# A first mixture with its elementwise steps laid out one by one, its differences on VectorE, and x loaded a second time, moved by a token

## The chip, the cores and the metric

The kernel runs on one core of one Trainium2 chip. The metric is device time in microseconds (us) of one launch. Engines: TensorE (PE; PEld is its weight load), VectorE (DVE), ScalarE (ACT), GpSimd (POOL), and SyncE (SP), whose queue issues most transfers.

## The reference, cut to what matters

```
attn  = relu(z zT / S)**2 @ v;  x = u * attn          # 4 x 3072 tokens, 256 wide
x_prev = x moved by one token, zero at the start of each sequence
xk = mu_k * x + (1 - mu_k) * x_prev
xr = mu_r * x + (1 - mu_r) * x_prev
k  = relu(xk @ w_k);  y = sigmoid(xr @ w_r) * (k * k @ w_v)   # the first mixture, 1024 wide inside
out = ((y @ w_a) * (y @ w_b)) @ w_out                  # the second mixture, 1536 wide inside
```

Everything is fp32 in and out. Weights arrive as 64-bit floats and are decoded in the kernel.

## The kernel before

Three stages follow each other: the attention, the first mixture, the second mixture. TensorE multiplies in fp32r, and each fp32 factor is split into a rounded part (hi) and a rest (lo), so that one product is three matmuls (hi hi, hi lo, lo hi: `mm3`, and the loop in `product`). A split is a copy to fp32r (`hi`, ScalarE) and a difference (`lo`, VectorE).

Tokens are taken in blocks of QB = 512 (24 of them; `i`), and the first mixture in pairs of blocks (NP = 12; `j`). The product with w_k of a pair is done by seven products in place of eight (`PRODUCTS`): the four blocks of xk (b11, b21 of the first token block, b12, b22 of the second) and four differences t1 to t4 (`value` in `operands`, tile `tv`) are split into seven `k_t` operands. A pair has UN = 4 units (`unit(u)`), each with 128 x 2 of the 1024 inner columns. A unit has seven products on PSUM banks `px`, `pw`, `py` (21 matmuls), the sums of banks that give `c1` and `c2`, relu and square, their splits (`kh`, `kl`), one gate (`gate`, bank `pg`, 6 matmuls, then a sigmoid), and, one unit later, four `net` calls (24 matmuls) that multiply k*k by w_v into four accumulators `vacc`. `result` multiplies them by the gate and stores y. A full unit thus has 51 matmuls; the first has no nets of a unit before it.

`net` 0 and 1 need the halves of `c1`, `net` 2 and 3 those of `c2`.

All of it is issued in an order written by hand (`tc.manual_schedule`): each engine and each DMA queue runs its instructions in the order of the program, and waits by semaphores for tiles. The elementwise work that prepares pair j + 1 is hung into the units of pair j: `side[(u, t)]` holds functions that `tick(t)` calls at eight places of unit u. Before, `steps` puts whole lists there, one entry per tick: `key_values` (xk: ScalarE forms (1 - mu) * x_prev by a copy with a scale, lines L523 and L525 for the column from the block before, VectorE adds mu * x, L530), `operands`, and `gate_values` (the same for xr, then the split `mix`). GpSimd (`SIDE`) computes the differences `tv` (L746) and the `lo` of `mix` (L569). For pair 0 the same work is hung into the end of the attention (`at(base - 22 + n, ...)`; the index counts half-units, and `base` is where the mixture begins).

Storage: `gp` (`g_tile`) has 25 buffers of 4 KB per partition for weights, operands of pair 0, x, the gates and half of the `mix` tiles, and for the attention's tiles ahead of that; `late` (`late_tile`) 18; `wp` (`w_tile`) 6, for `c1`, `c2`, `kh`, `kl`; `cp` (`c_tile`) 5 of 2 KB; `stp` 3; PSUM 4 banks `ps` and 4 accumulators. A tile takes a buffer when one is free, and its first writer waits for the last reader of the tile that had it.

The second mixture has 144 units of 33 matmuls, and prepares each next pair of blocks by the same `operands`, one list of steps per unit from its sixth unit on.

Of the kernel before, what the change touches and what calls it, by code (L numbers as in the profile page):

```python
# [16 lines left out]
P = 128  # L17
# [8 lines left out]
TICKS = 8  # L26
# [3 lines left out]
def tile_kernel(  # L30
# [60 lines left out]
    om = const.tile([P, 2, ND], F32, name="om")  # L91
# [19 lines left out]
    SIDE = nc.gpsimd  # L111
# [389 lines left out]
    mix_t, xk_t, k_t, sig_t = {}, {}, {}, {}  # L501
# [9 lines left out]
    def x_load(i):  # L511
        b, s = divmod(i, NQB)
        x_t[i] = g_tile([P, ND, QB], F32, "xs")
        nc.sync.dma_start(x_t[i], x_kept[b][:, :, s * QB : (s + 1) * QB])

    def mixed(i, c, d, dst):

        st = {}

        def before():  # L520
            x = x_t[i]
            st["t"] = t = c_tile(F32, "mt")
            nc.scalar.activation(t[:, 1:], x[:, d, : QB - 1], AF.Copy, scale=om[:, c, d : d + 1])  # L523
            if i % NQB:
                nc.scalar.activation(t[:, 0:1], x_t[i - 1][:, d, QB - 1 :], AF.Copy, scale=om[:, c, d : d + 1])  # L525
            else:
                nc.vector.memset(t[:, 0:1], 0.0)

        def both():
            nc.vector.scalar_tensor_tensor(  # L530
                dst(), x_t[i][:, d, :], mu[:, c, d : d + 1], st["t"], op0=ALU.mult, op1=ALU.add
            )

        return before, both

    def key_values(i):


        def dst(d):
            def fn():  # L540
                if d == 0:
                    xk_t[i] = stp.tile([P, ND, QB], F32, tag="st", name="xk")
                return xk_t[i][:, d, :]

            return fn

        (b0, m0), (b1, m1) = (mixed(i, 0, d, dst(d)) for d in range(ND))
        return [[b0], [m0, b1], [m1]]

    def gate_values(i):  # L550

        make = late_tile if i % 2 else g_tile
        st = {}

        def dst(d):
            def fn():
                if d == 0:
                    st["m"] = stp.tile([P, ND, QB], F32, tag="st", name="xr")
                return st["m"][:, d, :]

            return fn

        def high():
            mix_t[i] = [make([P, ND, QB], F32R, f"mix{h}") for h in range(2)]
            nc.scalar.activation(mix_t[i][0], st["m"], AF.Copy)

        def low():
            hi, lo = mix_t[i]
            SIDE.tensor_tensor(lo, st["m"], hi.bitcast(F32), op=ALU.subtract)  # L569

        (b0, m0), (b1, m1) = (mixed(i, 1, d, dst(d)) for d in range(ND))
        return [[b0], [m0, b1], [m1], [high], [low]]

    def mixture1():
        side = {}
        back = {}

        def steps(u, first, todo):
            for n, fns in enumerate(todo):
                v, t = divmod(first + n, TICKS)  # L580
                side.setdefault((u + v, t), []).extend(fns)

        def gate(u):

            j, f = divmod(u, UN)
            i, g = 2 * j + f // ND, f % ND
# [4 lines left out]
            pg = ps_tile("pg")  # L591
# [3 lines left out]
            nc.scalar.activation(sig_t[i][:, g, :], pg, AF.Sigmoid)  # L595

        def net(u, k):
# [6 lines left out]
            for d in range(ND):  # L604
# [469 lines left out]
```

## Time and profile before

| what | value |
|---|---|
| median of 3 runs | 2637.17 us (2634.65 to 2638.5) |
| the profiled execution | 2636.18 us, its span 2634.3 us |
| mean granted clock of TensorE | 0.998 |
| busy: PE, DVE, ACT, POOL | 99%, 74%, 63%, 11% |
| attention, first mixture, second mixture | 0 to 963, 963 to 1532, 1532 to 2634 us of the span |

A busy PE is not one at its peak, since matmuls overlap; the distance from one instruction's start to that of the next is the better measure. Idle time of another engine matters only where TensorE waits for it.

### The profile page before, as it was taken

What the parts mean: (1) busy time and instruction counts of PE and PEld (TensorE: products, weight loads), DVE (VectorE), ACT (ScalarE), POOL (GpSimd) and SP (SyncE); (2) the same over time, 40 slices, a digit from 0 to 9 for tenths busy, and PEclk for the clock granted to TensorE, in tenths of its full rate; (3) what the DMA queues carried; (4) which work ended last, traced back from release to release, by engine and by line L of the source; (5) the groups of instructions that cost most, each with busy time, mean ns of one, the idle gap of its engine ahead of it and who ended that gap; (6) DMA issues with size and microseconds to landing.
All of it is one profiled execution on the core that took longest, in us unless ns stands there. A gap on an engine that the chain in (4) does not pass through costs nothing.

```text
span 2634.3 us, 31196 instructions
## 1 busy us (share of the span) xinstructions
PE 2599.1 (99%) x11424; PEld 2132.1 (81%) x11424; DVE 1958.0 (74%) x2723; ACT 1665.3 (63%) x2380; POOL 281.8 (11%) x249
## 2 busy tenths in 40 slices
PE   8999999999999999999999999999999999999998
PEld 6888888888888877778878788888888888888887
DVE  7887877778778778788787767766676767677665
ACT  7867876787687667777777644444544444444443
POOL 0000100001001022222222200000000000000000
PEclk9999999999999999999999999999999999999999
DMA  7787779768968860110101340011011101110100
GB/s 208 210 231 187 222 222 235 209 188 251 214 182 240 222 178 33 49 48 33 64 32 36 137 172 25 9 33 33 1 33 32 33 1 32 33 25 9 32 17 17
DMA packets 254681, 274.14 MB, mean 104 GB/s; under 512 B 173632, under 2 KB 185920, under 8 KB 246848
## 3 DMA queue, kind: packets, MB, share of 16 engines
q1 hardware_dynamic: 234704, 175.68, 27.5%
q0 software_dynamic: 17712, 95.95, 9.5%
q8 instruction: 89, 1.46, 0.2%
q10 hardware_dynamic: 2112, 0.52, 0.1%
q14 instruction: 64, 0.52, 0.1%
HBM read 151.00 MB, written 121.11 MB: 103 GB/s over the span
## 4 chain that ended last, share of the span: by engine, by line
PE 88%; DVE 5%; ACT 2%; issue 2%; DMA 1%; SPq 0%; DVEq 0%; ACTq 0%
PE px L864 14%; PE acc L103 9%; PE acc L104 9%; PE acc L105 9%; PE py L864 7%; PE oacc L104 5%; PE oacc L105 5%; PE oacc L103 5%; PE pw L864 3%; PE px L631 3%; PE sc L357 3%; PE sc L358 3%; PE vacc L104 2%; PE vacc L105 2%; PE vacc L103 2%; PE py L631 2%
## 5 line engine op out<-in xcount | busy, mean ns | idle before, releaser
L104 PE MATMUL acc<-lo,vhi 128*128 128x512 f32 x1152 | 449.2, 390 | 1.6 <-DVE lo L419 1.6
L103 PE MATMUL acc<-hi,vhi 128*128 128x512 f32 x1152 | 450.0, 391 | 0.0
L105 PE MATMUL acc<-hi,vlo 128*128 128x512 f32 x1152 | 449.1, 390 | 0.0
L864 PE MATMUL px<-t,w 128*128 128x512 f32 x1296 | 364.2, 389 | 0.1
L848 ACT ACTIVATE abh<-cc 128x512 fp32r<-128x512 f32 x288 | 182.5, 634 | 282.8 <-DVE cc L930 254.1
L864 PEld LDWEIGHTS px<-t,w 128*128 128x128 f32 x1296 | 243.1, 188 | 51.4 <-ACT c L906 0.5
L924 DVE TENSOR_TENSOR c<-py,c 128x512 f32<-128x512 f32 x144 | 99.5, 691 | 235.9 <-ACT c L906 235.9
L104 PEld LDWEIGHTS acc<-lo,vhi 128*128 128x128 f32 x1152 | 216.7, 188 | 47.6 <-DVE lo L419 2.3
L105 PEld LDWEIGHTS acc<-hi,vlo 128*128 128x128 f32 x1152 | 216.6, 188 | 45.2
L103 PEld LDWEIGHTS acc<-hi,vhi 128*128 128x128 f32 x1152 | 216.7, 188 | 44.9
L370 ACT ACTIVATE p<-sc 128x1024 f32<-128x1024 f32 x167 | 171.1, 1024 | 117.2 <-PE sc L358 115.4
L377 DVE STREAM_TRANSPOSE pt<-p 128x512 f32<-128x512 f32 x240 | 156.4, 690 | 106.6 <-ACT p L371 102.1
L104 PE MATMUL oacc<-abl,w 128*128 128x512 f32 x572 | 223.7, 391 | 5.7 <-DVE abl L849 5.7
L105 PE MATMUL oacc<-abh,w 128*128 128x512 f32 x572 | 222.7, 389 | 0.0
L103 PE MATMUL oacc<-abh,w 128*128 128x512 f32 x572 | 222.6, 389 | 0.0
L906 ACT ACTIVATE c<-px 128x512 f32<-128x512 f32 x144 | 86.0, 597 | 214.7 <-PE px L864 214.7
L849 DVE TENSOR_TENSOR abl<-cc,abh 128x512 fp32r<-128x512 f32 x288 | 211.8, 736 | 0.1
L419 DVE TENSOR_TENSOR lo<-p,hi 128x1024 fp32r<-128x1024 f32 x167 | 199.6, 1195 | 5.1 <-PE pz L265 0.5
L371 ACT ACTIVATE p<-p 128x1024 f32<-128x1024 f32 x167 | 177.1, 1061 | 5.3
L419 DVE TENSOR_TENSOR lo<-pm,hi 128x1024 fp32r<-128x1024 f32 x120 | 147.1, 1227 | 33.1 <-ACT hi L416 32.7
L930 DVE SCALAR_TENSOR_TENSOR cc<-px,cc 128x512 f32<-128x512 f32 x144 | 99.5, 691 | 93.9 <-PE px L864 93.9
L104 PE MATMUL vacc<-kl,w 128*128 128x512 f32 x384 | 151.0, 393 | 0.5 <-DVE kl L641 0.5
(131 smaller groups left out, 5289.1 us busy)
## 6 DMA issues: line engine op xcount, KB each, us to landing
pkept<-pt POOLq DMA_DIRECT2D x60, 1024.0 KB, 5.9
pm<-pkept SPq DMA_DIRECT2D x240, 256.0 KB, 6.1
kept<-w POOLq DMA_DIRECT2D x39, 512.0 KB, 5.5
w<-kept SPq DMA_DIRECT2D x39, 512.0 KB, 8.6
vst<-in_v SPq DMA_DIRECT2D x24, 512.0 KB, 7.3
ust<-in_u SPq DMA_DIRECT2D x192, 64.0 KB, 4.4
xkept<-x POOLq DMA_DIRECT2D x24, 512.0 KB, 5.3
xs<-xkept SPq DMA_DIRECT2D x24, 512.0 KB, 5.6
```

Of the source, the lines that this page charges most:

```text
L103: nc.tensor.matmul(ps, wh, ah, start=first, stop=False)
L104: nc.tensor.matmul(ps, wh, al, start=False, stop=False)
L105: nc.tensor.matmul(ps, wl, ah, start=False, stop=last)
L370: nc.scalar.activation(p, sc, AF.Relu, scale=1.0 / S)
L371: nc.scalar.activation(p, p, AF.Square)
L377: nc.vector.transpose(pt[:, :, 2 * pr + t, :], p[:, t, :].rearrange("p (c i) -> p c i", i=SQ))
L419: nc.vector.tensor_tensor(l, p, h.bitcast(F32), op=ALU.subtract)
L631: nc.tensor.matmul(bank, w[x][:, c], t[:, y, :], start=first and m == 0, stop=end and m == 2, skip_group_check=True)
L848: return (lambda: nc.scalar.activation(h, p, AF.Copy)), (lambda: nc.vector.tensor_tensor(l, p, h.bitcast(F32), op=ALU.subtract))
L849: lambda: nc.vector.tensor_tensor(l, p, h.bitcast(F32), op=ALU.subtract)
L864: nc.tensor.matmul(bank, w[x][:, c], t[:, y, :], start=first and m == 0, stop=end and m == 2, skip_group_check=True)
L924: nc.vector.tensor_tensor(c22, y, c22, op=ALU.add)
```

## The change

In the first mixture:
- x of a block is loaded twice, as it is (`xs`) and moved by one token (`xp`; zero in the first column of a sequence). `change` takes xp from xs in place, and `mixed` forms xp + mu * (x - xp) in one VectorE instruction for each half. The copies with a scale (L523, L525) and the tile `om` go.
- `prepare(j)` lists every step with the unit and the tick at which it is issued. For pair 0 the 32 steps follow each other, one per half-unit, from `base - 33`.
- The differences `tv` and the `lo` of `mix` move from GpSimd to VectorE. `operands`, shared with the second mixture, changes in the same way there.
- In a unit, the order of work between the products changes (gate first, then nets by three, three and two). `c12` and `c22` are tiles of `cp`; bank y is copied by ScalarE after product 5, and x7 is added to it in one VectorE instruction. Relu, square and split of `c2` are issued in the next unit (`late`). The casts `kh` move from VectorE to ScalarE.
- The banks are asked for in an order that turns with the unit (`BANKS`).
- The gates of pair 0 all stand in unit 0, three of them on accumulators; sigmoids are issued some steps after their gate.

```diff
...
-    om = const.tile([P, 2, ND], F32, name="om")
...
-    SIDE = nc.gpsimd
...
+    mix_t, xk_t, xr_t, k_t, sig_t, p_t = {}, {}, {}, {}, {}, {}
...
     def x_load(i):
...
+        x_t[i], p_t[i] = (g_tile([P, ND, QB], F32, n) for n in ("xs", "xp"))
...
+        if s:
+            nc.sync.dma_start(p_t[i], x_kept[b][:, :, s * QB - 1 : (s + 1) * QB - 1])
+        else:
+            nc.vector.memset(p_t[i][:, :, 0:1], 0.0)
+            nc.sync.dma_start(p_t[i][:, :, 1:], x_kept[b][:, :, : QB - 1])
+    def change(i):
+        nc.vector.tensor_tensor(x_t[i], x_t[i], p_t[i], op=ALU.subtract)
+    def mixed(i, c, d):
+        t = (xk_t, xr_t)[c]
+        if d == 0:
+            t[i] = stp.tile([P, ND, QB], F32, tag="st", name=("xk", "xr")[c])
+        nc.vector.scalar_tensor_tensor(
+            t[i][:, d, :], x_t[i][:, d, :], mu[:, c, d : d + 1], p_t[i][:, d, :], op0=ALU.mult, op1=ALU.add
+        )
+    def gate_high(i, make):
+        mix_t[i] = [make([P, ND, QB], F32R, f"mix{h}") for h in range(2)]
+        nc.scalar.activation(mix_t[i][0], xr_t[i], AF.Copy)
+    def gate_low(i):
+        hi, lo = mix_t[i]
+        nc.vector.tensor_tensor(lo, xr_t[i], hi.bitcast(F32), op=ALU.subtract)
...
     def mixture1():
...
+        sigmoid = []
+        BANKS = (("px", "pw", "py", "pg"), ("pg", "px", "py", "pw"), ("pw", "pg", "py", "px"))
+        def gate(u, f, bank):
+            i, g = 2 * (u // UN) + f // ND, f % ND
...
+            pg = bank or accp.tile([P, QB], F32, tag="acc", name="vacc")
...
+            sigmoid.append(lambda: nc.scalar.activation(sig_t[i][:, g, :], pg, AF.Sigmoid))
+        def net(u, k, d):
...
+            first, last = f == 0 and k < 2, f == UN - 1 and k > 1
+            if first:
+                acc[n, d] = accp.tile([P, QB], F32, tag="acc", name="vacc")
+            c = slice(f * D + d * P, f * D + (d + 1) * P)
+            mm3(acc[n, d], wh[:, c], wl[:, c], hi, lo, first, last)
+            if last and d == ND - 1:
...
+            if prev < 0:
+                between = [[lambda g=g: gate(u, g, None if g else pg)] for g in range(UN)]
+            else:
+                nets = [lambda k=k, d=d: net(prev, k, d) for k in range(4) for d in range(ND)]
+                if j:
+                    between = [[lambda: gate(u, f, pg)], nets[:3], nets[3:6], nets[6:]]
+                else:
+                    between = [nets[:2], nets[2:4], nets[4:6], nets[6:]]
+            def gap(n):
+                for fn in between[n]:
+                    fn()
...
+            banks = {n: ps_tile(n) for n in BANKS[u % len(BANKS)]}
+            x, w, y, pg = (banks[n] for n in ("px", "pw", "py", "pg"))
+            relu, square, high, low = back[prev]["late"] if prev >= 0 else [lambda: None] * 4
             product(x, 1, True, False)
             product(w, 2, True, True)
...
             product(y, 5, True, False)
...
+            relu()
+            c1 = w_tile(F32, "c1")
+            c12, c22 = c_tile(F32, "c12"), c_tile(F32, "c22")
             nc.scalar.activation(c1[:, 0, :], x, AF.Copy)
             nc.vector.tensor_tensor(c1[:, 0, :], w, c1[:, 0, :], op=ALU.add)
+            square()
+            nc.scalar.activation(c22, y, AF.Copy)
             tick(0)
...
+            gap(0)
+            high()
             tick(1)
             product(x, 6, False, False)
-            nc.scalar.activation(c2[:, 0, :], x, AF.Copy)
+            nc.scalar.activation(c12, x, AF.Copy)
+            low()
+            if sigmoid:
+                sigmoid.pop(0)()
             tick(2)
...
+            gap(1)
+            while sigmoid:
+                sigmoid.pop(0)()
             tick(3)
             product(x, 7, False, False)
-            nc.scalar.activation(c1[:, 1, :], x, AF.Copy)
-            nc.vector.tensor_tensor(c1[:, 1, :], y, c1[:, 1, :], op=ALU.add)
+            nc.vector.tensor_tensor(c1[:, 1, :], x, c22, op=ALU.add)
             tick(4)
...
+            nc.scalar.activation(c1, c1, AF.Relu)
+            nc.scalar.activation(c1, c1, AF.Square)
+            gap(2)
+            while sigmoid:
+                sigmoid.pop(0)()
             tick(5)
             product(x, 4, False, True)
             product(y, 3, False, True)
...
+            c2 = w_tile(F32, "c2")
             nc.scalar.activation(c2[:, 1, :], x, AF.Relu)
...
+            h1 = w_tile(F32R, "kh")
+            nc.scalar.activation(h1, c1, AF.Copy)
+            nc.vector.tensor_tensor(c2[:, 0, :], y, c12, op=ALU.add)
             tick(6)
...
-            nc.vector.tensor_copy(h1, c1)
...
+            l1 = w_tile(F32R, "kl")
+            nc.vector.tensor_tensor(l1, c1, h1.bitcast(F32), op=ALU.subtract)
+            gap(3)
+            while sigmoid:
+                sigmoid.pop(0)()
             tick(7)
...
-            nc.vector.tensor_copy(h2, c2)
...
+            def relu():
+                nc.scalar.activation(c2[:, 0, :], c2[:, 0, :], AF.Relu)
+            def square():
+                nc.scalar.activation(c2, c2, AF.Square)
+            def high():
+                h = back[u]["h2"] = w_tile(F32R, "kh")
+                nc.scalar.activation(h, c2, AF.Copy)
+            def low():
+                h, l = back[u]["h2"], w_tile(F32R, "kl")
+                nc.vector.tensor_tensor(l, c2, h.bitcast(F32), op=ALU.subtract)
+                hl[0, 1], hl[1, 0] = (h[:, 0, :], l[:, 0, :]), (h[:, 1, :], l[:, 1, :])
...
+            back[u]["late"] = relu, square, high, low
...
+                for fn in back[u]["late"]:
+                    fn()
+                for k in range(4):
+                    flush.append(lambda k=k: [net(u, k, d) for d in range(ND)])
+        def prepare(j):
+            i0, i1 = 2 * j, 2 * j + 1
+            value, hi, lo = operands(k_t, j, lambda n: xk_t[2 * j + n], late_tile if j else g_tile)
+            odd = late_tile if j else g_tile
+            return [
+                (0, 0, lambda: change(i0)),
+                (0, 1, lambda: mixed(i0, 0, 0)),
+                (0, 3, lambda: mixed(i0, 0, 1)),
+                (1, 1, lambda: change(i1)),
+                (1, 1, hi["b11"]),
+                (1, 2, lambda: mixed(i1, 0, 0)),
+                (1, 3, lambda: mixed(i1, 0, 1)),
+                (1, 3, hi["b21"]),
+                (1, 4, value["t1"]),
+                (1, 5, lo["b11"]),
+                (1, 5, hi["t1"]),
+                (1, 6, value["t2"]),
+                (1, 7, lo["t1"]),
+                (2, 0, value["t4"]),
+                (2, 0, hi["t2"]),
+                (2, 1, lo["b21"]),
+                (2, 1, hi["t4"]),
+                (2, 2, value["t3"]),
+                (2, 2, hi["b22"]),
+                (2, 3, lo["t2"]),
+                (2, 3, hi["t3"]),
+                (2, 4, lo["t4"]),
+                (2, 5, lo["b22"]),
+                (2, 6, lo["t3"]),
+                (3, 0, lambda: mixed(i0, 1, 0)),
+                (3, 1, lambda: mixed(i0, 1, 1)),
+                (3, 2, lambda: mixed(i1, 1, 0)),
+                (3, 2, lambda: gate_high(i0, g_tile)),
+                (3, 3, lambda: mixed(i1, 1, 1)),
+                (3, 4, lambda: gate_high(i1, odd)),
+                (3, 5, lambda: gate_low(i0)),
+                (3, 6, lambda: gate_low(i1)),
+            ]
...
+        at(base - 40, lambda: x_load(0))
+        at(base - 39, lambda: x_load(1))
+        for n, (_, _, fn) in enumerate(prepare(0)):
+            at(base - 33 + n, fn)
+        at(base - 3, lambda: x_load(2))
+        for j in range(1, NP):
...
+            if j > 1:
+                side.setdefault((u - 1, 4), []).append(lambda j=j: x_load(2 * j))
+            side.setdefault((u, 4), []).append(lambda j=j: x_load(2 * j + 1))
+            for v, t, fn in prepare(j):
+                side.setdefault((u + v, t), []).append(fn)
+        u = (NP - 1) * UN
+        side.setdefault((u, 4), []).append(lambda: y_load(0))
+        value, hi, lo = operands(t_t, 0, lambda n: y_t[0][n], lambda *a: (g_tile if a[2] == "b22" else late_tile)(*a))
+        for v, t, fn in (
...
+        ):
+            side.setdefault((u + v, t), []).append(fn)
...
     def operands(t_t, j, source, make):
...
-                SIDE.tensor_tensor(val[name], a(), b(), op=ALU.subtract)
+                nc.vector.tensor_tensor(val[name], a(), b(), op=ALU.subtract)
...
+        return {"t1": t1, "t2": t2, "t3": t3, "t4": t4}, hi, lo
...
+                value, hi, lo = operands(
...
+                steps = [
+                    [value["t1"], hi["b11"], hi["t1"]],
+                    [lo["b11"], lo["t1"], hi["b21"]],
+                    [value["t2"], lo["b21"], hi["t2"]],
+                    [lo["t2"], value["t4"], hi["t4"]],
+                    [lo["t4"], value["t3"], hi["t3"]],
+                    [lo["t3"], hi["b22"]],
+                    [lo["b22"]],
+                ]
...
```

## Rows read from the trace of the kernel before

**Rows 1.** The page, part 1: busy us, share of the span, instructions.
```profile
PE 2599.1 (99%) x11424; PEld 2132.1 (81%) x11424; DVE 1958.0 (74%) x2723; ACT 1665.3 (63%) x2380; POOL 281.8 (11%) x249
```

**Rows 2.** Two products on `pw`, one unit apart (timeline, PE: start, us, what).
```profile
1200.01 0.84 PE L631 MATMUL pw<-b,w 128*128 128x512 f32 x3
1211.57 0.84 PE L631 MATMUL pw<-b,w 128*128 128x512 f32 x3
```

**Rows 3.** Stretches: us, busy (instructions) of PE, PEld, DVE, ACT, POOL; PEclk, DMA, GB/s.
```profile
963.50:1009.24 45.74, 43.38 (x181) 34.37 (x180) 33.59 (x42) 37.80 (x62) 12.13 (x7) 0.96 0.18 58
1009.24:1533.04 523.80, 516.39 (x2246) 417.00 (x2244) 417.47 (x524) 398.87 (x647) 124.09 (x65) 1.00 0.17 58
1152.62:1200.01 47.39, 46.87 (x206) 37.92 (x204) 38.05 (x48) 36.74 (x62) 11.49 (x6) 1.00 0.14 45
1533.04:1544.27 11.23, 10.53 (x46) 8.37 (x45) 7.25 (x11) 2.45 (x5) 0.00 (x0) 1.00 0.24 89
1544.27:2615.22 1070.95, 1065.28 (x4688) 878.73 (x4686) 738.50 (x1116) 495.76 (x831) 63.97 (x44) 1.00 0.12 29
```

**Rows 4.** The end of the attention on PE (timeline; in brackets the idle time before).
```profile
954.71 0.50 PE L104 MATMUL acc<-lo,vhi 128*128 128x512 f32 x1 [1.56 <-DVE lo L419]
```

**Rows 5.** The wait in a usual pair (timeline, all engines).
```profile
1181.09 3.37 POOL L746 TENSOR_TENSOR tv<-xk,tv 128x512 f32<-128x512 f32 x2 [2.51 <-DVE xk L530]
1181.54 1.79 DVE L760 TENSOR_TENSOR t<-tv,t 128x512 fp32r<-128x512 f32 x1
1183.25 0.68 DVE L668 TENSOR_TENSOR c<-py,c 128x512 f32<-128x512 f32 x1
1183.98 0.50 PE L631 MATMUL py<-b,w 128*128 128x512 f32 x1 [0.53 <-DVE c L668]
```

**Rows 6.** The `lo` differences of `tv` (by tile: ns least/median/most).
```profile
L760 DVE TENSOR_TENSOR t<-tv,t x96: 637/683/1790, 936.8 to 2520.6; 128x512 fp32r<-128x512 f32 x96
```

**Rows 7.** The wait in the second mixture (timeline, all engines).
```profile
1738.45 3.00 POOL L746 TENSOR_TENSOR tv<-y,tv 128x512 f32<-128x512 f32 x2
1740.21 1.78 DVE L849 TENSOR_TENSOR abl<-cc,abh 128x512 fp32r<-128x512 f32 x1
1742.05 0.50 PE L104 MATMUL oacc<-abl,w 128*128 128x512 f32 x1 [0.27 <-DVE abl L849]
```

**Rows 8.** Waits of the second mixture: us in sum, times, longest.
```profile
PEld oacc L104 <- DVE abl L849: 9.9, 10, 1.8
```

**Rows 9.** Waits of the first mixture: us in sum, times, longest.
```profile
ACT c L659 <- DVE kl L641: 61.1, 33, 3.5
```

**Rows 10.** The `lo` of `c1` and `c2` (by tile: ns least/median/most).
```profile
L641 DVE TENSOR_TENSOR kl<-c,kh x96: 1224/1225/2197, 973.6 to 1534.2; 128x1024 fp32r<-128x1024 f32 x96
```

**Rows 11.** Groups of the first mixture: busy us, mean ns | idle before.
```profile
L523 ACT ACTIVATE mt<-xs,om 128x511 f32<-128x511 f32 x90 | 64.2, 714 | 2.7 <-DMA xs<-xkept 2.7
L683 DVE CAST kh<-c 128x1024 fp32r<-128x1024 f32 x47 | 32.8, 698 | 27.5 <-ACT c L678 27.5
L667 ACT ACTIVATE c<-px 128x512 f32<-128x512 f32 x48 | 28.5, 594 | 15.9 <-PE px L631 15.9
L565 ACT ACTIVATE mix<-xr 128x1024 fp32r<-128x1024 f32 x23 | 24.3, 1057 | 3.1 <-DVE xr L530 3.1
```

**Rows 12.** The page, part 6: transfers, KB each, us to landing.
```profile
xs<-xkept SPq DMA_DIRECT2D x24, 512.0 KB, 5.6
```

**Rows 13.** Unit 0 of the first mixture (timeline, ACT and PE).
```profile
967.15 1.28 ACT L595 ACT_TABLE_LOAD   x1
969.58 0.73 PE L631 MATMUL px<-t,w 128*128 128x512 f32 x2 [1.84 <-ACT c L667]
```

**Rows 14.** Waits of SP's queue, 900 to 1020 us: us in sum, times, longest.
```profile
SPq L234 <- PE acc L105: 12.0, 2, 7.2
```

More of the change, by code (lines that the diff above doesn't have):

```diff
@@ L536, in key_values @@
[L536 to L572, printed above, removed]
+        if s:
[3 more added lines that the diff above has]
+            nc.sync.dma_start(p_t[i][:, :, 1:], x_kept[b][:, :, : QB - 1])
@@ L603, in net @@
             wh, wl = weights["v", row]
-            for d in range(ND):
-                first, last = f == 0 and k < 2, f == UN - 1 and k > 1
-                if first:
-                    acc[n, d] = accp.tile([P, QB], F32, tag="acc", name="vacc")
-                c = slice(f * D + d * P, f * D + (d + 1) * P)
-                mm3(acc[n, d], wh[:, c], wl[:, c], hi, lo, first, last)
-            if f == UN - 1 and k > 1:
+            first, last = f == 0 and k < 2, f == UN - 1 and k > 1
[4 more added lines that the diff above has]
+            if last and d == ND - 1:
                 result(j, n, acc)
@@ L693, in unit @@
             hl[0, 0], hl[1, 1] = (h1[:, 0, :], l1[:, 0, :]), (h1[:, 1, :], l1[:, 1, :])
-            hl[0, 1], hl[1, 0] = (h2[:, 0, :], l2[:, 0, :]), (h2[:, 1, :], l2[:, 1, :])
+            back[u]["late"] = relu, square, high, low
             if u == NP * UN - 1:
-                flush.extend(lambda k=k: net(u, k) for k in range(4))
-        base = len(units)
-        for j in range(NP):
-            i0, i1 = 2 * j, 2 * j + 1
-            ops = operands(k_t, j, lambda n, j=j: xk_t[2 * j + n], g_tile if j == 0 else late_tile)
-            if j == 0:
-                at(base - 34, lambda: (x_load(0), x_load(1)))
-                for n, step in enumerate(key_values(0) + key_values(1) + ops + gate_values(0)):
-                    for fn in step:
-                        at(base - 22 + n, fn)
-                steps(0, 1, gate_values(1))
-                continue
-            u = (j - 1) * UN
-            side.setdefault((u, 7), []).extend([lambda i0=i0: x_load(i0), lambda i1=i1: x_load(i1)])
-            steps(u + 1, 3, key_values(i0))
-            steps(u + 1, 6, key_values(i1))
-            steps(u + 2, 2, ops)
-            steps(u + 3, 1, gate_values(i0))
-            steps(u + 4, 1, gate_values(i1))
@@ L716, in mixture1 @@
-        ends = operands(t_t, 0, lambda n: y_t[0][n], lambda *a: (g_tile if a[2] == "b22" else late_tile)(*a))
-        side.setdefault(((NP - 1) * UN, 4), []).append(lambda: y_load(0))
-        steps((NP - 1) * UN + 2, 1, ends)
+                for fn in back[u]["late"]:
[40 more added lines that the diff above has]
+            ]
@@ L1022, in tile_kernel @@
         in_turn(0, *v_prep(0, 0))
-        at(NKT, lambda: nc.vector.tensor_scalar(om, mu, -1.0, 1.0, op0=ALU.mult, op1=ALU.add))
         last = max(len(units), max(sides) + 1)
```

84 lines of the change are left out of this document (18 added, 66 removed).

## The prediction

> **What bounds the kernel now.** I read the page first: TensorE is busy 99% of the span [rows 1]. That alone says little, because matmuls overlap, so I read their pace next. In a unit of the first mixture that nothing disturbs, two starts of `pw` lie 11.56 us apart with 51 matmuls between them [rows 2]: 0.2267 us each, weight loads included. Neither kernel has more or fewer matmuls than the other, so the floor is fixed, and what a change can win is the time that TensorE loses against that pace, stage by stage [rows 3]:
>
> - Pair 0 of the first mixture (180 matmuls, 40.80 us) takes 45.74: 4.94 lost.
> - Pairs 1 to 11 (204 matmuls each, 11 x 46.24 = 508.64 us) take 523.80: **15.16 lost**, some 1.15 in a usual pair.
> - The first unit of the second mixture (45 matmuls, 10.20 us) takes 11.23: 1.03 lost.
> - The next 142 units (33 matmuls, 7.48 us each, 1062.16) take 1070.95: **8.79 lost**.
>
> Together 29.9 us; the end of the attention loses 1.6 more in one wait [rows 4]. Then I asked what stands in front of each loss. In the first mixture [rows 5] TensorE waits for VectorE's add at L668, which frees `py` for product 3. That add is late because a difference of 512 columns just before it took 1.79 us while GpSimd ran a `tv` difference; the usual time of that line is 0.683 [rows 6]. In the second mixture it is the same [rows 7]: `abl` takes 1.78 us while GpSimd computes `tv`, and TensorE waits for it, 10 times in all [rows 8], once for each later pair. So both large losses have one origin: VectorE instructions more than double while GpSimd works on its tensors. A second, smaller one: ScalarE's copy at L659 waits 61 us in sum [rows 9], because `c2` must take over a buffer that the last `kl` of the unit before still reads.
>
> **The change, part by part.**
>
> *Differences from GpSimd to VectorE.* Per pair VectorE gets four `tv` differences at 0.683 [rows 6], two `change` and two `gate_low` of 1024 columns at 1.224 (the least in row L641) [rows 10]: +7.6 us. It loses eight casts `kh` at 0.698 [rows 11]: -5.6. It also no longer has its slow cases: I take 3 us (four L760 at 1.2 instead of 0.68, and one or two `kl` at 2.1 instead of 1.22). Busy time of a pair goes from 38.05 [rows 3] to about 37 of 46.24. Worth, if nothing else is late: in the second mixture all of 8.79 but a remainder of 0.3, since the places where `tv` now stands come after the second `abl` of a unit, where rows of before already show two VectorE differences without a wait of TensorE; the `y` loads stay three units ahead. In the first mixture it is the greater part of 15.16.
>
> *x loaded a second time, moved by a token.* Eight ScalarE copies of 0.714 per pair vanish [rows 11] (and their one-column companions); 24 transfers of 512 KB are added, median 5.6 us to landing [rows 12]. In steady state they are issued by SP behind the `y` stores, more than half a pair before `change` reads them. DMA share there is 0.14 [rows 3]. I take nothing; without that cover one transfer late would hold VectorE, and TensorE some 2 us after, by at most 6 us per pair.
>
> *Casts `kh` to ScalarE, the copy of x7 replaced by one of y5.* +2 x 1.057 per unit [rows 11], +8.5 us per pair, against 5.7 and about 2 removed. ScalarE stays near 37 of 46.24.
>
> This edit moves work to the slower engine: the cast of 1024 columns takes VectorE 0.698 and ScalarE's copy of the same size 1.057 [rows 11]. If ScalarE set the end of the first mixture, the 96 casts would cost 96 x 0.36 = 34.5 us there, and the total would be 2636.2 - 8.5 + 34.5 = 2662. It does not come to that as long as the deadlines below are met; what it would take is the third rival. A page speaks against the edit in the same sense. The Trainium skill, "VectorE: DVE Perf Modes", section "Mode 2×_2P — use both read ports for one tensor", says that an operation with one source in SBUF, such as a copy, runs at two elements per cycle even in fp32, while one on two tensors cannot; by that rule the edit takes from VectorE just the work that it does cheaply. The trace agrees with the rule: 0.698 for the cast, 1.224 for the difference of the same width.
>
> *The order of a unit.* I walked one unit of pairs 1 to 11 by hand, at 0.2267 per matmul, ScalarE 0.594 for a bank, 1.057 for 1024 columns, VectorE 0.69 and 1.22 [rows 6, 10, 11], and 0.2 from a product's last matmul to its reader. TensorE: products 1, 2, 5 to 2.04 us; gate to 3.40; product 6 to 4.08; three nets to 6.12; product 7 to 6.80; three nets to 8.84; products 4, 3 to 10.20; two nets to 11.56. What each of these waits for, and when it comes:
> - product 6 at 3.40 needs the copy of bank x: done 1.5;
> - product 7 at 6.12 needs the copy `c12`: done 4.9, or 5.6 in the unit with two operand copies ahead of it;
> - product 4 at 8.84 needs the add of x7 (one add, no ScalarE copy before it as now): 7.7;
> - product 3 needs only the copy of y5: 3.0. This is the wait of rows 5, and it is gone;
> - nets 0 to 3 from 4.08 of the next unit need `l1`: add 7.7, relu 8.8, square 9.9, relu of bank x 10.4, cast 11.3 to 11.8, difference by 13.4 at worst, that is 1.8 of the next unit: slack 2.3;
> - nets of `h2`, `l2` from 7.5 of the next unit: difference done by 5.8: slack 1.7;
> - product 5 of the next unit needs `y` free (add done at 11.1, wanted at 12.9): slack 1.8. The turned order of banks hands `px` to a bank read long before.
>
> The least slack is 0.5 to 1.1 us, so I expect next to no loss; I keep 1.5 us for all pairs, bounds 0 and 6. The 8.79 and the 15.16 are thus 8.5 and 13.7 of gain.
>
> *The start.* This is where I am least sure. Before, unit 0 loses time through a table load of 1.28 us in front of a copy that product 4 waits for, 1.84 idle [rows 13], and a lower clock behind it (0.96 for the pair). After, unit 0 has four gates (45 matmuls), so product 4 no longer meets the load, but `l1` of unit 0 comes at about 12.9 for a net that could start at 12.24: 0.7 lost, some 0.4 after it. Against it stands storage. Pool `gp` has 25 buffers. In unit 0 there live 12 weight tiles, 7 operands, 4 `mix` (two of them came from another pool before) and 2 x tiles: 25 already, and `sig` twice and the next x pair want four more. SP, ScalarE and VectorE therefore wait for attention tiles and `mix` tiles to come free, as SP already does before, 12.0 us in two waits of the weight loads [rows 14]. I follow it: `mix` of block 0 is free 5.6 us into unit 0, that of block 1 at 10.4; then x of block 3 would land at 16 to 17 and its `change` would hold VectorE, and the `low` behind it, for 1 to 3 us. I put the loss of pair 0 at 5 us, as before, with bounds 1 and 13. The 32 preparing steps of pair 0 start 33 half-units before the end of the attention instead of 22, on VectorE without GpSimd; the 1.6 lost there [rows 4] may go, or become 3. Net of both: 0, from -5 to +9.
>
> *First unit of the second mixture.* Four `sig` products still stand there: no change from 1.03.
>
> *The sum.* The profiled execution of before took 2636.18 (span 2634.30 and 1.88 around it), 1 us under the median 2637.17. 2636.18 - 13.7 - 8.5 + 0 = **2614**.
>
> **The rivals.**
> 1. *Storage at the start costs what it can.* For it: 29 tiles for 25 buffers; and a stall of about 2 us lowered the clock before. Against it: matmuls queued three units ahead. It gives 2614 + 9 = 2623.
> 2. *The first mixture keeps its loss.* The walk is wrong somewhere by a microsecond (two engines at 80% in fixed order), and a new wait, likely of nets 0 and 1 for `l1` or of product 7 for `c12`, costs as much as the old. Only the second mixture gains: 2636.2 - 8.5 = 2628.
> 3. *ScalarE's order becomes the bound (slower).* Each unit has 8.9 us of ScalarE work without side steps, strung on a chain relu, square, cast. If the chain passed its slack of 2.3 us, `l1` would come late in every unit. From some 0.5 us per unit on (48 units, 24 us) this eats the gains of both mixtures (13.7 + 8.5); priced by the casts alone, 0.36 us each and two per unit, on top of the loss of before, it gives 2636.2 - 8.5 + 34.5 = 2662. Against it: ScalarE is to be busy some 80%, and waits for PSUM now.
> 4. *Nothing moves*, because VectorE's slow cases come from something else than GpSimd. Every slow row that I looked at overlaps a `tv` or `mix` of GpSimd, so this is nearly excluded.
>
> **The numbers.** A measurement tells about 0.2% (5.3 us). Chances: the forecast 0.64 (2605 to 2620), rival 1 0.14 (2618 to 2627), rival 2 0.11 (2623 to 2633, a quarter of it within 0.2%), rival 3 0.07, rival 4 and smaller mixtures 0.04. Faster 0.87, same 0.06, slower 0.07. The range 2606 to 2628 reaches from nearly the full 29.9 us to rival 2's middle.
>
> **What would show it.** Right: pairs 1 to 11 take 508.6 to 511 us; the units of the second mixture all 7.48; L760 and `kl` with one duration (0.68, 1.22); GpSimd empty of tensor work; no wait of `py` for L668. Wrong: a row of TensorE waiting for `kl`, `c12` or `h2` once per unit; VectorE waiting for the DMA of `xs` or `xp` in every pair; more than 8 us lost in pair 0 with ScalarE's `sig` or `mix` waiting for a buffer.

## The result, and the profile after

The changed kernel takes 2609.18 us (median of 4 runs, 2608.67 to 2609.6) against 2636.47 (4 runs, 2634.65 to 2638.5) on the same chip: ratio 0.9896, 95% interval 0.9879 to 0.9913. The forecast of 2614 was 4.8 us too high; the time lies inside the stated range, 2606 to 2628.

The page's part 1 [rows 1], and the transfers of x [rows 12]:

```profile
PE 2585.4 (99%) x11424; PEld 2135.3 (82%) x11424; DVE 1943.8 (75%) x2758; ACT 1681.3 (64%) x2300; POOL 72.8 (3%) x129
...
xs<-xkept SPq DMA_DIRECT2D x24, 512.0 KB, 5.8
```

TensorE is as busy as before and has the same matmuls; GpSimd is left with 3%. The gain shows in the stretches only. These are the stretches of [rows 3], with the same columns, cut at the same `pw` products:

```profile
959.77:1004.29 44.52, 42.73 (x181) 33.23 (x180) 31.94 (x42) 36.39 (x51) 0.68 (x1) 1.00 0.38 130
1004.29:1512.93 508.64, 508.64 (x2245) 421.17 (x2244) 394.25 (x509) 416.93 (x584) 0.00 (x0) 1.00 0.21 76
1512.93:1525.20 12.27, 10.78 (x46) 8.29 (x45) 6.57 (x10) 4.06 (x6) 0.00 (x0) 1.00 0.22 82
1525.20:2587.44 1062.24, 1062.24 (x4688) 879.48 (x4686) 746.83 (x1160) 496.05 (x831) 0.00 (x0) 1.00 0.11 29
```

Taken against the pace of 0.2267 us per matmul, as the prediction did, TensorE loses:

| stretch | before | after |
|---|---|---|
| pair 0 | 4.94 | 3.72 |
| pairs 1 to 11 | 15.16 | 0.00 |
| first unit of the second mixture (the seam) | 1.03 | 2.07 |
| its next 142 units | 8.79 | 0.08 |

The profiled execution took 2608.67 us, 27.5 less than before: 15.2 from pairs 1 to 11, 8.7 from the second mixture, 1.2 from pair 0, 2.4 from the end of the attention (the wait of [rows 4] is gone), 1.4 that was there already at 880 us, ahead of the first load that the change moves (the kernels built on the changed one show 0.4 to 3.3 at this place, so it tells nothing of the change), less 1.0 in the seam unit and 0.3 behind the last unit.

The durations that were spread in [rows 6] and [rows 10], here as groups by shape (busy us, mean ns, then idle before); the first two are of pairs 1 to 11, the third of the second mixture:

```profile
L680 DVE TENSOR_TENSOR kl<-c,kh 128x1024 fp32r<-128x1024 f32 x44 | 53.8, 1224 | 10.2 <-ACT kh L676 10.2
...
L809 DVE TENSOR_TENSOR t<-tv,t 128x512 fp32r<-128x512 f32 x44 | 30.1, 684 | 1.2 <-ACT t L802 1.1
...
L890 DVE TENSOR_TENSOR abl<-cc,abh 128x512 fp32r<-128x512 f32 x284 | 193.9, 683 | 0.0
```

The means now equal the usual durations of before, 1.224 and 0.683. TensorE has no wait at all in pairs 1 to 11 and in the 142 units. What is left stands in pair 0 and in the seam unit (timeline, PE):

```profile
972.83 0.50 PE L102 MATMUL vacc<-kl,w 128*128 128x512 f32 x1 [0.76 <-DVE kl L662]
...
979.42 0.96 PE L593 MATMUL px<-t,w 128*128 128x512 f32 x3 [0.48 <-DVE c L645]
...
1515.24 0.96 PE L905 MATMUL px<-t,w 128*128 128x512 f32 x3 [0.79 <-ACT cc L922]
...
1523.72 0.96 PE L905 MATMUL py<-b,w 128*128 128x512 f32 x3 [0.70 <-DVE c L965]
```

### The profile page after: what moved, and what is told of

It is laid out like the page before. It is cut to its first block, busy times and chain, and to the rows that moved or that the text cites. A ratio compares the mean times of both kernels' runs of the same rounds, so it can differ in the third digit from the quotient of the medians.

```text
span 2606.8 us, 30823 instructions
## 1 busy us (share of the span) xinstructions
PE 2585.4 (99%) x11424; PEld 2135.3 (82%) x11424; DVE 1943.8 (75%) x2758; ACT 1681.3 (64%) x2300; POOL 72.8 (3%) x129
## 4 chain that ended last, share of the span: by engine, by line
PE 97%; DMA 1%; ACT 1%; DVE 0%; issue 0%; SPq 0%; DVEq 0%; ACTq 0%
PE px L905 15%; PE acc L101 10%; PE acc L103 10%; PE acc L102 10%; PE py L905 7%; PE oacc L101 5%; PE oacc L102 5%; PE oacc L103 5%; PE px L593 5%; PE pw L905 4%; PE vacc L102 3%; PE vacc L101 3%; PE vacc L103 3%; PE sc L354 3%; PE sc L355 3%; PE py L593 2%
## 5 line engine op out<-in xcount | busy, mean ns | idle before, releaser
L965 DVE TENSOR_TENSOR c<-py,c 128x512 f32<-128x512 f32 x144 | 99.7, 692 | 219.4 <-ACT c L947 219.4
L890 DVE TENSOR_TENSOR abl<-cc,abh 128x512 fp32r<-128x512 f32 x288 | 196.6, 683 | 0.1
```

The costliest lines, as they stand in the source:

```text
L890: lambda: nc.vector.tensor_tensor(l, p, h.bitcast(F32), op=ALU.subtract)
L965: nc.vector.tensor_tensor(c22, y, c22, op=ALU.add)
```

## The experiments

Each was profiled and timed beside the kernel before; "loss" is again against TensorE's pace. Together:

| run | us | ratio, 95% interval | pair 0 | pairs 1–11 | seam | 142 units |
|---|---|---|---|---|---|---|
| e1_differences_only | 2638.81 | 1.0016 (1.0006–1.0025) | 5.86 | 23.40 | 1.02 | 0.02 |
| e2_all_but_differences | 2618.23 | 0.9934 (0.9919–0.9949) | 3.76 | 0.00 | 2.10 | 7.86 |
| e3_casts_on_vector | 2608.95 | 0.9902 (0.9887–0.9917) | 4.32 | 0.01 | 1.04 | 0.05 |
| e4_banks_fixed | 2610.47 | 0.9905 (0.9888–0.9921) | 5.07 | 0.00 | 2.10 | 0.06 |
| e5_nets_first | 2618.69 | 0.9936 (0.9922–0.9951) | 4.20 | 8.90 | 1.96 | 0.02 |
| e6_scaled_copies | 2629.77 | 0.9981 (0.9972–0.9991) | 8.77 | 15.82 | 2.08 | 0.08 |
| e7_gpsimd_every_unit | 2693.98 | 1.0223 (1.0208–1.0238) | 3.48 | 0.00 | 2.10 | 85.45 |
| e8_start | 2610.89 | 0.9907 (0.9890–0.9923) | 5.13 | 0.00 | 2.08 | 0.05 |
| e9_seam | 2606.58 | 0.9894 (0.9877–0.9910) | 3.59 | 0.00 | 0.00 | 0.10 |
| e10_start_and_seam | 2608.53 | 0.9899 (0.9884–0.9914) | 5.58 | 0.00 | 0.00 | 0.06 |
| e11_difference_later | 2607.09 | 0.9889 (0.9874–0.9904) | 4.03 | 0.00 | 0.00 | 0.01 |
| e12_square_at_once | 2620.06 | 0.9938 (0.9926–0.9951) | 6.40 | 9.11 | 2.08 | 0.00 |

### One half of the change at a time

e1 is the kernel before with its differences on VectorE and nothing else:

```diff
-    SIDE = nc.gpsimd
+    SIDE = nc.vector
```

> The kernel before, with the differences tv and the rest of mix on VectorE in place of GpSimd, and nothing else of the change. Theory (GpSimd's tensor work slows VectorE, and that is where nearly all of the lost time comes from): the second mixture loses 0 to 0.5 instead of 8.8 us, pairs 1 to 11 lose 0 to 5 instead of 15.2, the end of the attention loses 0 to 1 instead of 2.4; total 2612 to 2620 us. Rival (the old order of the first mixture is too tight for VectorE to take 7.6 us more per pair, so it keeps its loss and only the second mixture gains): 2625 to 2630 us.

The second mixture did what both mixtures were to do: 0.02 lost. The first lost more than before, 23.40, 22.5 of it in the fourth unit of each pair, 13.5 us long where 11.56 is the pace. The longest sum among TensorE's waits in pairs 1 to 11 of the kernel before (us in sum, times, longest), then both waits there of e1, and VectorE and ScalarE ahead of one of them (timeline):

```profile
PE py L631 <- DVE c L668: 5.2, 10, 0.5
```

```profile
PE vacc L104 <- DVE kl L641: 8.4, 11, 0.8
PE vacc L103 <- DVE kh L683: 6.7, 11, 1.2
```

```profile
1040.44 0.69 DVE L668 TENSOR_TENSOR c<-py,c 128x512 f32<-128x512 f32 x1 [0.31 <-ACT c L667]
1041.05 0.68 DVE L746 TENSOR_TENSOR tv<-xk,tv 128x512 f32<-128x512 f32 x1
...
1041.76 0.64 ACT L753 ACTIVATE t<-tv 128x512 fp32r<-128x512 f32 x1 [1.36 <-DVE tv L746]
...
1043.76 0.63 ACT L753 ACTIVATE t<-tv 128x512 fp32r<-128x512 f32 x1 [0.88 <-DVE tv L746]
1044.30 1.05 ACT L675 ACTIVATE c<-c 128x1024 f32<-128x1024 f32 x1
...
1046.80 0.69 DVE L683 CAST kh<-c 128x1024 fp32r<-128x1024 f32 x1 [1.08 <-ACT c L678]
```

No difference is slow here, and the ten waits for L668, of which [rows 5] show one, are gone: the third unit of a pair, where they stood, loses 0.6 us in sum over pairs 1 to 11 instead of 8.9. So the prediction had read this wait rightly. But `tv` now stands in VectorE's queue behind an add that waits for ScalarE, and ScalarE's queue stands at the copy of `tv` with the unit's relu behind it. The relu starts 2.2 us of idle time later, and `kh` and `kl` come late to the net: the fourth units lose 22.5 instead of 3.1. GpSimd beside VectorE is not needed for this new loss. The end of the attention, which was to gain, lost 1.5 more.

e2 is the other half: the changed kernel with those differences on GpSimd again.

```diff
-                nc.vector.tensor_tensor(val[name], a(), b(), op=ALU.subtract)
+                nc.gpsimd.tensor_tensor(val[name], a(), b(), op=ALU.subtract)
...
-        nc.vector.tensor_tensor(lo, xr_t[i], hi.bitcast(F32), op=ALU.subtract)
+        nc.gpsimd.tensor_tensor(lo, xr_t[i], hi.bitcast(F32), op=ALU.subtract)
```

> The changed kernel with the differences tv and the rest of mix back on GpSimd, all else of the change kept. Theory: the second mixture loses its 8.7 us again; in the first, VectorE's slow cases of 1 to 1.1 us come back, and the slack of 0.5 to 1.8 us that the new order has takes up part of them, so pairs 1 to 11 lose 2 to 15 us; total 2620 to 2633 us. Rival (the new order alone is what removed the loss of the first mixture): its units stay at 11.56 us, only the second mixture loses, 2616 to 2619 us.

The second mixture loses 7.86 again, pairs 1 to 11 nothing, as the rival had it. VectorE's groups that are slow beside GpSimd in pairs 1 to 11, first in the kernel before, then in e2, and TensorE's wait in the second mixture of e2:

```profile
L641 DVE TENSOR_TENSOR kl<-c,kh 128x1024 fp32r<-128x1024 f32 x89 | 120.0, 1348 | 5.7 <-DVE kh L691 0.5
L760 DVE TENSOR_TENSOR t<-tv,t 128x512 fp32r<-128x512 f32 x44 | 51.9, 1181 | 0.0
...
L760 DVE TENSOR_TENSOR b<-xk,b 128x512 fp32r<-128x512 f32 x30 | 25.3, 845 | 0.1
```

```profile
L662 DVE TENSOR_TENSOR kl<-c,kh 128x1024 fp32r<-128x1024 f32 x45 | 58.1, 1292 | 13.2 <-ACT kh L658 13.1
...
L809 DVE TENSOR_TENSOR t<-tv,t 128x512 fp32r<-128x512 f32 x44 | 30.1, 684 | 1.4 <-ACT t L802 1.4
...
L809 DVE TENSOR_TENSOR b<-xk,b 128x512 fp32r<-128x512 f32 x30 | 28.4, 947 | 0.0
```

```profile
PE oacc L102 <- DVE abl L890: 4.7, 10, 1.3
```

In the first mixture some of VectorE's `lo` are slow again beside GpSimd (947 ns in place of 687 in the changed kernel), and the new order takes them without a wait of TensorE. But it also meets fewer of them. Against 1224 and 685 ns, these groups took 37.6 us too long in the kernel before and 10.9 in e2, where the `lo` of `tv`, the slow row of [rows 5], no longer lies beside GpSimd. So the two losses have two cures: the order alone is enough in the first mixture, the differences alone in the second. How much of the first cure is room for late steps, and how much is that steps no longer meet GpSimd, these runs don't separate.

### How much a neighbour on GpSimd costs

e7 adds to each unit of the second mixture three differences on GpSimd whose output nothing reads.

```diff
                 back[u]["p"] = {0: c11, 1: c12}
+                dz = c_tile(F32, "dz")
+                for _ in range(3):
+                    nc.gpsimd.tensor_tensor(dz, c11, c11, op=ALU.subtract)
```

> The changed kernel with three GpSimd differences of 512 columns added to every unit of the second mixture; they read c11 and write a tile that nobody reads, so they carry no data to anyone and only run beside VectorE. Theory (they slow VectorE by their mere running): abl at 1.2 to 1.8 us instead of 0.68, TensorE loses 0.3 to 1.7 us in each of 144 units, total 2650 to 2850 us. Rival (the loss of before came from waiting for the values that GpSimd made, or for its buffers): 2608 to 2612 us.

The units went from 7.48 to between 8.05 and 8.15 us, but for one of 7.77. One unit, GpSimd, then VectorE (timeline), then TensorE's wait in the 142 units:

```profile
1703.03 1.04 POOL L977 TENSOR_TENSOR dz<-cc 128x512 f32<-128x512 f32 x1 [4.22 <-DVE cc L971]
1704.15 1.37 POOL L977 TENSOR_TENSOR dz<-cc 128x512 f32<-128x512 f32 x1
1705.60 1.37 POOL L977 TENSOR_TENSOR dz<-cc 128x512 f32<-128x512 f32 x1
...
1703.60 1.02 DVE L973 SCALAR_TENSOR_TENSOR cc<-cc,c 128x512 f32<-128x512 f32 x1
1704.54 1.52 DVE L890 TENSOR_TENSOR abl<-cc,abh 128x512 fp32r<-128x512 f32 x1
1705.99 0.68 DVE L927 TENSOR_TENSOR cc<-pw,cc 128x512 f32<-128x512 f32 x1
1706.59 0.92 DVE L890 TENSOR_TENSOR abl<-cc,abh 128x512 fp32r<-128x512 f32 x1
```

```profile
PE oacc L102 <- DVE abl L890: 40.5, 141, 0.3
```

While GpSimd works, `abl` takes 1.52 us and L973 1.02, where 0.683 and 0.692 are their times alone; both read two tiles in SBUF. L927, which reads one of its two tiles from PSUM, lies beside the third GpSimd difference and keeps its 0.68. The slow ones are not slow throughout, they wait: L973 and both `abl` end 0.55 us after the end of the GpSimd difference that ran when they started (1704.07, 1705.52, 1706.97). So do 141 of 141 L973 in these units, and in the kernel before all 30 L760 of pairs 1 to 11 and all 19 `abl` that start while GpSimd works on `tv` (0.545 to 0.554 us). The Trainium skill, "SBUF — State Buffer", section "Who interferes with whom", says which of them meet: a VectorE instruction with two SBUF inputs contends with a GpSimd instruction that reads SBUF, and one with at most one, outside the modes that use both ports, does not. This trace agrees, by L973 and `abl` on one side and L927 on the other.

### What in the new order matters

Five parts of the new layout were undone singly, in the changed kernel. e3 puts the casts `kh` on VectorE again; e4 asks for the banks in one fixed order.

```diff
-            nc.scalar.activation(h1, c1, AF.Copy)
+            nc.vector.tensor_copy(h1, c1)
...
-                nc.scalar.activation(h, c2, AF.Copy)
+                nc.vector.tensor_copy(h, c2)
```

> The changed kernel with the casts kh on VectorE again (0.70 us each in place of 1.06 on ScalarE). Theory of deadlines (both engines have slack in every unit): 2608 to 2611 us, no unit longer than 11.56. Rival (VectorE is nearly full, and the move to ScalarE is what made room): units grow by 0.1 to 0.5 us each, 2613 to 2635 us. The page that calls the copy cheap on VectorE would have it faster than the changed kernel, by up to 3 us at the start and the seam.

```diff
-        BANKS = (("px", "pw", "py", "pg"), ("pg", "px", "py", "pw"), ("pw", "pg", "py", "px"))
+        BANKS = (("px", "pw", "py", "pg"),)
```

> The changed kernel with px, pw, py, pg asked for in the same order in every unit, so that product 1 meets the bank that the unit before read last. Theory of deadlines: the relu of bank x is done at 10.4 to 10.9 of 11.56 us, so product 1 waits in no unit; 2608 to 2611 us. Rival (the turned order is needed): 0.1 to 0.5 us per unit, 2613 to 2633 us, with TensorE waiting in px for that relu.

Neither loses anything in pairs 1 to 11: both engines have room for the casts, and the turned banks are worth nothing that shows there. e3 even halves the seam's loss, 1.04 for 2.07, but loses 0.6 more in pair 0. Pair 0 of e4 lost 1.35 more than the changed kernel's; that goes with a late load, as shown below, and is not shown to come from the banks.

e5 puts two groups of nets ahead of the gate:

```diff
-                    between = [[lambda: gate(u, f, pg)], nets[:3], nets[3:6], nets[6:]]
+                    between = [nets[:2], nets[2:4], [lambda: gate(u, f, pg)], nets[4:]]
```

> The changed kernel with the order of before between the products: two nets, two nets, the gate, four nets, in place of the gate first. By the walk, nets 0 and 1 then want l1 at 2.04 us of the unit instead of 4.08, and l1 comes at 0.8 to 1.8, with 0.1 to its reader: theory, a loss of 0 to 0.3 us in the unit where it is latest and none elsewhere, 2608 to 2614 us. Rival (the late l1 sets the pace as soon as the gate does not stand before it): 0.3 us or more in each of 44 units, 2622 us and up.

8.90 us lost, between the theory and its rival, and not at the place of either: no net waits for `l1`. Ahead of product 4 there are now two groups of six matmuls behind product 6 where there were two of nine, so it comes six matmuls, 1.36 us, sooner. In the second unit of each pair (12.27 us) it waits (timeline, PE, then VectorE's queue ahead of it):

```profile
1212.34 0.96 PE L593 MATMUL px<-t,w 128*128 128x512 f32 x3 [0.41 <-DVE c L645]
```

```profile
1208.00 1.22 DVE L521 TENSOR_TENSOR xs<-xs,xp 128x1024 f32<-128x1024 f32 x1
1209.13 1.22 DVE L680 TENSOR_TENSOR kl<-c,kh 128x1024 fp32r<-128x1024 f32 x1
1210.27 1.41 DVE L528 SCALAR_TENSOR_TENSOR xk<-xs,mu,xp 128x512 f32<-128x512 f32 x2
1211.59 0.69 DVE L645 TENSOR_TENSOR c<-px,c 128x512 f32<-128x512 f32 x1
```

The add that frees the bank stands behind 3.6 us of VectorE work from start to start, 2.5 of it for the next pair. The prediction's walk has this add done at 7.7 and product 4 at 8.84. In e5 product 4 is due at 7.48; product 7 comes 0.68 sooner too, so the add could be done at 7.0, but behind that queue it is done 8.0 us into the unit, which started at 1204.28.

e6 takes the second load of x and the difference away; ScalarE forms x_prev * (1 - mu) by scaled copies again, at the new places.

```diff
-        nc.vector.tensor_tensor(x_t[i], x_t[i], p_t[i], op=ALU.subtract)
...
+        m = c_tile(F32, "mt")
+        nc.scalar.activation(m[:, 1:], x_t[i][:, d, : QB - 1], AF.Copy, scale=om[:, c, d : d + 1])
```

> The changed kernel without the second load of x: the moved half of xk and xr is formed by ScalarE's copies with a scale as before, each directly ahead of the VectorE instruction that adds to it. ScalarE's work per pair rises from 38 to about 45 of 46.24 us busy. Theory: in fixed order that does not fit, l1 comes after its deadline in the units with side copies, 0.5 to 2 us in two of four units, 2620 to 2650 us. Rival (the second load is not needed): below 2612 us.

15.82 lost, as much as the first mixture had gained, all of it in the fourth units of pairs 1 to 10, and not for `l1`. There TensorE waits for the add of x7, and VectorE's queue ahead of it for ScalarE's copies (timeline, PE and VectorE):

```profile
1245.22 0.98 PE L595 MATMUL px<-t,w 128*128 128x512 f32 x3 [1.02 <-DVE c L647]
```

```profile
1243.81 0.75 DVE L530 SCALAR_TENSOR_TENSOR xr<-xs,mu,mt 128x512 f32<-128x512 f32 x1 [0.95 <-ACT mt L527]
1244.48 0.68 DVE L647 TENSOR_TENSOR c<-px,c 128x512 f32<-128x512 f32 x1
```

e12 issues the second half's relu, square, cast and difference at the end of their own unit:

```diff
-            back[u]["late"] = relu, square, high, low
+            for fn in (relu, square, high, low):
+                fn()
```

> Edit: the changed kernel with a unit's second relu, square, cast and difference issued at the end of that unit instead of between the first steps of the next one. Theory (what removes the first mixture's loss is the order in which ScalarE meets the steps that TensorE waits for): square and cast, 1.06 us each, now stand ahead of the copy that the fourth product of the next unit needs; by the changed kernel's timeline that copy ends 2.2 us after the unit's start and is needed at 3.4, so it would come 0.9 us late in every unit: 20 to 42 us lost in pairs 1 to 11, time 2630 to 2652 us. Rival (the engines have slack enough in any order, only GpSimd beside VectorE made steps late): pairs 1 to 11 lose under 2 us, time 2609 to 2611 us.

9.11 lost: the direction of the theory, under half of its least size. The third unit of most pairs pays 0.71, where two operand copies stand on ScalarE ahead of `c12`; the others next to nothing, but for 1.0 in the first unit of pair 1. The copy L626, which was to come at 4.3 us of a unit, comes at 3.5, wanted at 3.4. ScalarE in such a unit, whose first product starts at 1077.49 (timeline):

```profile
1078.37 1.06 ACT L672 ACTIVATE c<-c 128x1024 f32<-128x1024 f32 x1
1079.47 1.06 ACT L676 ACTIVATE kh<-c 128x1024 fp32r<-128x1024 f32 x1
1080.43 0.58 ACT L626 ACTIVATE c<-px 128x512 f32<-128x512 f32 x1
...
1083.02 0.63 ACT L801 ACTIVATE t<-tv 128x512 fp32r<-128x512 f32 x1 [1.00 <-DVE tv L794]
1083.56 0.58 ACT L635 ACTIVATE c<-px 128x512 f32<-128x512 f32 x1
```

### What is left: the start and the seam

e8 loads the sigmoid's table ahead of pair 0 and takes the first two `sig` tiles from another pool. e9 issues the last unit's relu, square and split inside the first unit of the second mixture, and frees `py` earlier there. e10 is both.

```diff
-                sig_t[i] = g_tile([P, ND, QB], F32, "sig")
+                sig_t[i] = (late_tile if i < 2 else g_tile)([P, ND, QB], F32, "sig")
...
+        at(base - 1, lambda: nc.scalar.activation(c_tile(F32, "warm")[:, 0:1], mu[:, 0, 0:1], AF.Sigmoid))
```

> The changed kernel with two edits at the start of the first mixture: a sigmoid of one column on ScalarE, one half-unit before the mixture, so that the table load lies in ScalarE's idle time, and the two sig tiles of pair 0 taken from the pool late instead of gp, so that two more buffers are free for x of block 3. Theory: the 0.76 us wait for kl in unit 1 shrinks by most of itself, the change of block 3 no longer waits 1.3 us for its transfer, the clock does not fall; pair 0 loses 0.5 to 2 us instead of 3.7, total 2606.5 to 2608.5 us. Rival (the waits of pair 0 come from the length of the chain and from the buffers that the weights of the nets wait for, and stay): 2608.5 to 2610 us.

```diff
-                for fn in back[u]["late"]:
-                    fn()
+                tail.extend(back[u]["late"])
...
+                if u == 0:
+                    nc.vector.tensor_tensor(c22, y, c22, op=ALU.add)
```

> The changed kernel with the seam between the mixtures laid out anew: relu, square, cast and rest of the last c2 are issued between the first copies of the second mixture instead of all ahead of them, and the add that frees py in its first unit stands ahead of the four sig products on VectorE. Theory: both waits of that unit (0.79 for the copy of bank x, 0.70 for py) and the slower matmuls behind them go, the unit takes 10.2 to 10.6 instead of 12.27 us, total 2607 to 2608.3 us. Rival (the last c2 comes too late for its nets then): the unit stays at 11.5 us or more, 2608.5 us and up.

> The changed kernel with the edits of the start (table load early, sig of pair 0 in the other pool) and of the seam together. They touch stages 550 us apart, so the gains should add: 2604.5 to 2607.5 us by the theories of both; 2608 us or more if neither wait was where I put it.

The seam edit works: 10.20 us, nothing lost. The start edit does not: pair 0 loses 5.13 in e8 and 5.58 in e10, and the gains don't add. The table load is out of the way and the wait for `kl` at L662 with it, but VectorE meets this in the second unit (timeline, of e8):

```profile
976.50 1.23 DVE L521 TENSOR_TENSOR xs<-xs,xp 128x1024 f32<-128x1024 f32 x1 [3.31 <-DMA xp<-xkept]
```

In the changed kernel the same line, at 975.08, waits 1.34. The load of the fourth block of x lands late, and the splits and adds behind it in VectorE's queue come late with it. What that load itself waits for (waits of SP's queue from 955 to 969.5 us, first in the changed kernel, then in e8):

```profile
SPq L231 <- DMA xkept<-x: 7.2, 1, 7.2
...
SPq L514 <- PE vacc L103: 0.8, 1, 0.8
```

```profile
SPq L231 <- DMA xkept<-x: 7.5, 1, 7.5
```

It stands behind a load of weights (L231) that waits for the attention's last x to be stored, and then, in the changed kernel, for the last gate to have read a `mix` tile. e8 removes only the second, shorter wait. Its `xp` is issued 9.14 instead of 9.49 us after the first `pw` of pair 0, but x of the next block is loaded right behind, and `xp` lands at 15.94 instead of 15.22; that the one slows the other is not shown. Where the landing differs by itself, the loss follows it: in e7, e9, the changed kernel, e2, e5 and e4 `xp` lands at 14.99, 15.10, 15.22, 15.28, 15.70 and 16.51, and pair 0 loses 3.48, 3.59, 3.72, 3.76, 4.20 and 5.07.

e11 is e9 with these steps three gaps later in pair 0:

```diff
-            for v, t, fn in prepare(j):
-                side.setdefault((u + v, t), []).append(fn)
+            for n, (v, t, fn) in enumerate(prepare(j)):
+                t += 8 * v + (3 if j == 1 and 3 <= n < 24 else 0)
+                side.setdefault((u + t // 8, t % 8), []).append(fn)
```

> Edit: the kernel of e9, and in the first pair alone the steps on the second slice's x (from its difference on) stand three gaps later. Theory from the traces of the changed kernel and of e8: in the second unit VectorE stands 1.34 us (e8: 3.31 us) at the difference of x for a load that lands late, and the adds and splits queued behind it come late to TensorE. Then pair 0 loses 0.8 to 1.5 us where e9 lost 3.59, and the time is 2604 us (2603 to 2605.5). Rival: the loss is ScalarE's order around the table load and the chain of splits, and the difference only shared the delay: pair 0 still loses 3.2 us or more, and the time stays at 2606.5 us.

Missed: pair 0 loses 4.03, and the time is no better than e9's. The four units of its pair 0 (stretches, columns as in [rows 3]):

```profile
958.15:968.35 10.20, 10.20 (x46) 8.45 (x45) 4.83 (x7) 6.66 (x9) 0.68 (x1) 1.00 0.72 242
968.35:979.99 11.64, 10.79 (x46) 8.37 (x45) 7.30 (x9) 10.24 (x16) 0.00 (x0) 1.00 0.31 106
979.99:990.80 10.81, 10.58 (x46) 8.29 (x45) 8.93 (x13) 9.29 (x15) 0.00 (x0) 1.00 0.00 0
990.80:1002.98 12.18, 11.10 (x47) 8.21 (x45) 10.98 (x14) 10.12 (x14) 0.00 (x0) 1.00 0.52 172
```

The second unit fell from e9's 12.89 to 11.64, as the theory had it, but the fourth rose from 10.22 to 12.18: VectorE is busy 10.98 of it, and TensorE waits there for `kl` (0.47) and for the add of x7 (0.50). The late load was a cause, and its cure moved the loss. A placement that avoids both was not tried.

The fastest median is e9's, 2606.58. By the ratios to the kernel before, 0.9894 against 0.9896, the whole time doesn't separate it from the changed kernel; its seam unit, 10.20 against 12.27, does.

## Why the prediction came out as it did

Its sum was 2614 where the profiled execution took 2608.67. Term by term:

- **Second mixture: right.** 8.7 of 8.79 gained where 8.5 was predicted, for the reason given: e2 brings the loss back by GpSimd alone, e7 makes it nearly tenfold, e1 removes it by the differences alone.
- **Pairs 1 to 11: the size right, 15.16 in place of 13.7; the wait read rightly, its cure credited wrongly.** The step that failed is to put the greater part of 15.16 down to the moved differences. e1 moved only these, and the loss grew to 23.40; e2 left them on GpSimd, and the loss was nil. So here they are neither enough nor needed, while the new order is enough. "Both large losses have one origin" holds for the waits of [rows 5], which went with the slow differences in e1; what the prediction didn't see is that in the order of before the moved `tv` makes a dearer wait, because steps that TensorE needs soon stand on ScalarE and VectorE behind steps on operands for the next pair. That the forecast of this stage came out is in part luck: its sum didn't depend on which half of the change earned it. The prediction's own walk of the order found no late step, and that came true, down to 0.00 of the 1.5 kept in reserve. Three parts of the new layout are shown to count, by e5, e6 and e12, 8.90, 15.82 and 9.11; these don't add up to 15.16. Casts and banks (e3, e4) count for nothing in these pairs.
- **The start: mis-sized by 3.6.** It was put at a net of nothing. The end of the attention gained 2.4 and pair 0 1.2. No `sig` or `mix` waited for a buffer as rival 1 had it; what came late was the x of block 3, by the path that the prediction had followed, with the weight loads ahead of it in SP's queue: it landed 15.9 us into unit 0 (16 to 17 predicted) and held VectorE for 1.34 us (1 to 3).
- **The seam unit: mis-sized by 1.0.** The prediction saw the `sig` products there and not that relu, square and split of the last unit, which the new order delays, are all issued at its end and stand on ScalarE ahead of the copy at L922. e9 moved them, and the add at L965 ahead of the `sig` products, and the whole loss went, the 1.03 that the prediction let stand included.
- 1.4 us of the difference to the forecast lies ahead of the change, and is luck.

Rivals 2 and 3 failed by the same numbers: no wait in pairs 1 to 11, ScalarE busy 417 us of 508.6. Rival 3's worry, that the casts go to the dearer engine, is answered by e3: their engine makes no difference in pairs 1 to 11.

## What to carry over

Before a gain is put down to one half of a change, make each half alone: the slow row stood right in front of the wait in both stages, but taking only it away was the whole cure in one stage and, in the other, moved work to a place in a queue where it cost more. Where two engines feed a third in fixed order, place each step by when its reader needs it and keep what is needed later behind it. At the ends of such a pipeline (first pair, last unit) walk the delayed steps once more; there they met work for which the steady state has room.

## What the runs showed of the hardware

- A wait of TensorE costs more than its row says. In e1 the rows name 15.1 us in pairs 1 to 11 where 23.4 were lost, in e5 4.1 of 8.90, in e12 1.1 of 9.11, in e7 40.5 of 85.45 in the 142 units. A loss is better read from the pace than from the sum of the waits.
- The wait of 1.84 us in pair 0 of before [rows 13] was followed by products of three matmuls that took 1.31, 1.28 and 1.00 us from start to start instead of 0.68; the granted clock there, from 970.5 to 973.5 us, was 0.50, the lower of the two levels (1.2 of 2.4 GHz). With the wait gone, so was that: the granted clock of the pair went from 0.96 to 1.00. In e8, behind its wait of 1.82 us for `kl`, it was 0.50 from 981 to 983.5 us; two products there took 1.44 and 1.28, which is 1.4 of the 5.0 us that its second unit lost.
